# Round 0 of an RWKV-6 kernel: levels 0 and 1 and the diagonal as quarter products on TensorE

## The chip, the cores and the metric

The kernel runs on one core of one Trainium2 chip. A core has five engines that run their own instruction lists side by side: TensorE (PE, matrix products; its weight loads are shown as PEld), VectorE (DVE), ScalarE (ACT), GpSimd (POOL) and SyncE (SP, which here only issues DMA transfers). The metric is the device time of one execution in microseconds, as a median over runs. One more execution was recorded by the hardware profiler; its trace is what the views below are taken from.

## The reference

Everything is fp32. Batch B = 4, heads H = 8, steps S = 768, head size D = 48. First a recurrence over the steps, one 48x48 state per head:

```python
for t in range(S):
    cur = einsum('bhd,bhe->bhde', u[None] * k_t, v_t)
    y[:, :, t] = einsum('bhd,bhde->bhe', r_t, state + cur)
    state = w_t[:, :, :, None] * state + einsum('bhd,bhe->bhde', k_t, v_t)
```

Then y is brought into the form (4, 768, 384), called x, and goes through layer norm (with the gain g), a product with w_ch1 (384x1536), relu, a product with w_ch2 (1536x384), and x is added.

Written out over a stretch of steps, the output at step t is a sum over earlier steps s of v_s times the number A[s, t] = sum over d of k_s[d] r_t[d] times all w[d] strictly between s and t; for s = t the factor is u[d] instead; and what came before the stretch comes in through the state. The kernel works in that form: A is the matrix that this change is about.

## The kernel before

*Rounds.* The 4x768 steps are cut into 8 rounds of 384 steps (three tiles of 128 steps, TT = 3), each with all 8 heads. Two heads lie together in one turned operand (rows 0 to 47 and 64 to 111), which gives two units of two pairs. Within a round A is built for chunks of 64 steps (C = 64); the decays are multiplied up over six levels (NLEV = 6) of blocks of 1, 2, 4, 8, 16 and 32 steps.

*What a level does.* At level n, A's entries between a block of 2^n steps and the block that follows it are one product of k, already multiplied by the w up to the end of its block, and r, already multiplied by the w from the start of its block. `quads` (line 807) computes these as small TensorE products, 64 rows by 32 columns in PSUM (tile `a`), four of them on the four quadrants of the array; `keep` (868) copies what belongs to the level into A with a mask (DVE, copy_predicated), and for the last level `keep_last` (895) does so on ACT; `grow` (839, DVE) multiplies k and r by the totals of w, so that they fit the next level; `totals` (784) makes these totals by products of pairs.

*Below level 2.* The quarter products start at level 2 (LOW = 2). What lies within a block of four steps, that is levels 0 and 1 and the diagonal with u, is made from the inputs as loaded ("natural": step on the partitions, no transposing), in `inner` (570): elementwise products on DVE or POOL of nat_k, nat_r and nat_w, and sums over d into `vals`. It also leaves k and r, multiplied up to level 2, in the padded tiles pad_k and pad_r, and the product of four w in `w4`. `turn` (728) transposes pad_k and pad_r (four transposes of 128x112 into one PSUM bank, evicted by ACT or DVE into k and r); `turn_w` (756) does so with `w4`, into `tot`. `inner_by_tile` (670) sends `vals` to DRAM (own_d) and fetches it back in the layout of A (`va`): seven small transfers on SP for each part of a round. `place_own` (705) puts `va` into A with a mask.

*After A.* `turn_k`, `load_v`, `states`, `inside`, `outputs` (912 to 1133) make the products with v and the chain of states; `normalize` and `turn_x` (1134, 1225) the layer norm and its transposes; `first_product`, `mlp`, `halve` and `thirds` (1568, 1594, 1358, 1471) the two products of the metaformer, with `h_ps` the PSUM of the first one. The first rounds use fp32 weights. Later rounds use weights and activations split into parts (tiles whose names carry H, L and D); `thirds` issues the last rounds' second product, and ends with two DVE additions and a store for each tile of 128 steps.

*Weights.* They arrive as 8-byte words (`raw`, 384 KB each, on SP's queue) and are made into fp32 by ACT and DVE (`convert`, 1289). The first product cannot start before the first of them are done.

*Round 0.* It has two parts: its first tile alone, and the two others (`parts_of_round`, 512). Nothing else can run yet, so TensorE waits in it. `front` (1688) writes down all work of a part.

*What sets the order.* Every step is handed to a planner (class `Plan`) as an operation with an estimated cost, what it reads and what it writes. The order in which operations are issued is written out by hand as a list of their numbers (`ORDER`, line 76; ten thousand times n added where the n-th alternative engine is to do it). Each engine runs its own share of that list in that order. The planner's costs don't change the order, they only tell where TensorE is expected to wait for more than 0.35 us:

```python
if idle and e == "PE" and t - free["PE"] > 0.35:
    early = max(min(t - 0.1, self.WARMED) - free["PE"], 0.0)
    n = int(early / idle[1] / 2 + (t - 0.1 - free["PE"] - early) / idle[1])
```

There it issues products of zeros, `idle` (1783), n units of 128 columns, up to three units in one instruction. They are instructions like any other: once in the list they run. `busy` (1792) holds the times at which each engine is taken to be free at first. One helper issues every instruction, so all rows of the profile carry its line, L47; tiles tell them apart.

Of the kernel before, what the change touches and what calls it, by code (L numbers as in the profile page):

```python
# [63 lines left out]
class Plan:  # L64
# [294 lines left out]
def kernel(  # L359
# [18 lines left out]
    P = 128  # L378
# [349 lines left out]
    def turn(nm, part, c, stage):  # L728
        rnd, c0, nc = part
        name, ps = f"{nm}{rnd}", f"{nm}_ps{rnd}_{c}"  # L730
        pad = f"pad_{nm}{rnd}"

        def go():
            t = tile_("b", ps, [P, Q * P])
# [953 lines left out]
    def front(part):  # L1688
# [27 lines left out]
        for c in range(c0, c0 + nc):  # L1716
            for nm in "kr":
                turn(nm, part, c, 4 + "kr".index(nm))
# [106 lines left out]
```

## Time and profile before

| | us |
|---|---|
| median of 3 runs | 469.41 (468.7 to 469.71) |
| the profiled execution, whole | 469.36 |
| its span (first to last recorded instruction) | 467.6 |
| TensorE busy | 459.7 (98%) |
| VectorE busy | 352.5 (75%) |
| ScalarE busy | 264.5 (57%) |
| GpSimd busy | 139.1 (30%) |

The span leaves out 469.36 − 467.6 = 1.76 us that lie around it. A row of the timeline gives the start, the time from the first start to the last end, engine, line, operation, `output<-inputs`, the moving shape and the number of records (an fp32 product leaves two), and in brackets how long the engine stood idle before and what released it. Tile names: `k_ps`, `r_ps`, `w_ps` the turned inputs, `a` the quarter products and the products with v, `xT_ps` the turned x, `h_ps` the first product, `idle` the products of zeros.

### The profile page before, as it was taken

The page shows a single profiled execution, that of the slowest core. Times are in us where ns is not written, and L with a number is a line of the kernel's source. Part 1 is how long each engine was busy: PE and PEld are TensorE (multiplying, and loading weights), DVE is VectorE, ACT ScalarE, POOL GpSimd, SP SyncE. Part 2 cuts the span into 40 slices and gives each one's busy share as a digit, 9 for nine tenths or more (in the row PEclk, how much of TensorE's full clock was granted, in tenths as well). Part 3 has the DMA queues.
Part 4 walks back from the last instruction along what each step waited for, and adds up shares of the span by engine and source line. Part 5 has one row for each costly group of instructions (what it writes and reads, how often), then busy time and mean ns, then how long its engine had stood idle before and what let it go on. Part 6 is the DMA issues. An engine that isn't in the chain of part 4 may idle for free.

```text
span 467.6 us, 17460 instructions
## 1 busy us (share of the span) xinstructions
PE 459.7 (98%) x7442; PEld 400.8 (86%) x7442; DVE 352.5 (75%) x742; ACT 264.5 (57%) x608; POOL 139.1 (30%) x141
## 2 busy tenths in 40 slices
PE   9999999999999999999999999999999999999996
PEld 5766888766899766899766899999999999999996
DVE  8999899999997768897879887976633535525535
ACT  4697889754674332665621678855555455544440
POOL 4237014322361152363443230221013122321030
PEclk9999999999999999999999999999999999999999
DMA  7889765885657606844630545312212232142011
GB/s 207 248 199 240 203 124 144 239 212 139 180 160 162 133 4 151 185 128 127 170 66 4 86 123 133 105 32 69 84 55 70 80 102 67 37 135 68 35 50 51
DMA packets 105501, 56.23 MB, mean 120 GB/s; under 512 B 61904, under 2 KB 102352, under 8 KB 105424
## 3 DMA queue, kind: packets, MB, share of 16 engines
q1 hardware_dynamic: 105152, 54.92, 45.9%
q8 instruction: 58, 0.95, 0.9%
q10 hardware_dynamic: 272, 0.20, 0.1%
q14 instruction: 19, 0.16, 0.1%
HBM read 45.27 MB, written 7.47 MB: 113 GB/s over the span
## 4 chain that ended last, share of the span: by engine, by line
PE 86%; DVE 6%; DMA 3%; ACT 2%; POOL 2%; issue 1%; DVEq 0%; SPq 0%; POOLq 0%; ACTq 0%
PE h_ps L47 28%; PE a L47 25%; PE o L47 15%; PE o_2P L47 4%; PE idle L47 3%; PE r_ps L47 2%; PE k_ps L47 2%; PE o_2D L47 2%; DMA raw<-in_moe_w_ch_dram 2%; PE kn_ps L47 2%; PE xT_ps L47 2%; DVE s L47 1%; ACT held L47 1%; DMA va<-own_d 1%; POOL nat_k L47 1%
## 5 line engine op out<-in xcount | busy, mean ns | idle before, releaser
L47 ACT ACTIVATE h<-h_ps 128x384 f32<-128x384 f32 (+2 forms) x108 | 47.9, 457 | 50.5 <-PE h_ps L47 49.8
L47 PE MATMUL o<-ffn,h 128*128 128x384 f32 x216 | 74.6, 491 | 0.0
L47 DVE SCALAR_TENSOR_TENSOR hD<-hH,hL 128x384 fp32r<-128x384 f32 x60 | 36.4, 617 | 37.1 <-POOL hL L47 16.0
L47 POOL TENSOR_TENSOR hL<-h,hH 128x384 fp32r<-128x384 f32 x28 | 30.2, 1084 | 102.7 <-PE a L47 27.7
L47 ACT ACTIVATE h_ps<-h_ps 128x384 f32<-128x384 f32 x84 | 39.7, 480 | 34.5 <-PE h_ps L47 33.4
L47 PEld LDWEIGHTS o<-ffn,h 128*128 128x128 f32 x216 | 39.2, 190 | 23.0
L47 PEld LDWEIGHTS a<-r,k 48*56 48x56 f32 (+3 forms) x3072 | 40.0, 122 | 10.8 <-issue 5.2
L47 PE MATMUL h_ps<-xd,d 128*128 128x384 f32 x204 | 47.1, 335 | 0.0
L47 PE MATMUL a<-r,k 48*56 48x32 f32 (+3 forms) x3072 | 44.2, 208 | 1.0 <-issue 0.7
L47 PE MATMUL h_ps<-xhl,wl 128*128 128x384 f32 x180 | 40.4, 334 | 0.0
L47 DVE TENSOR_TENSOR r<-r,tot 112x768 f32<-112x768 f32 (+1 forms) x40 | 32.3, 809 | 9.6 <-PE a L47 9.6
L47 PE MATMUL h_ps<-xhl,wh 128*128 128x384 f32 x180 | 39.1, 326 | 0.0
L47 DVE TENSOR_TENSOR k<-k,tot 112x768 f32<-112x768 f32 (+1 forms) x40 | 31.6, 791 | 6.7 <-PE a L47 4.7
L47 ACT ACTIVATE hH<-h 128x384 fp32r<-128x384 f32 x60 | 29.7, 519 | 11.6 <-PE a L47 7.8
L47 PEld LDWEIGHTS h_ps<-xd,d 128*128 128x128 f32 x204 | 34.0, 189 | 0.5
L47 DVE TENSOR_TENSOR hL<-h,hH 128x384 fp32r<-128x384 f32 x32 | 18.0, 569 | 20.0 <-PE a L47 9.5
L47 PEld LDWEIGHTS h_ps<-xhl,wh 128*128 128x128 f32 x180 | 30.8, 189 | 0.0
L47 PE MATMUL idle<-nought 128*128 128x384 f32 (+2 forms) x90 | 29.6, 452 | 0.9 <-DVE eps L47 0.9
L47 ACT COPY A<-a 32x384 f32<-32x384 f32 (+5 forms) x56 | 23.6, 422 | 11.9 <-DVE xhl L47 5.6
L47 PEld LDWEIGHTS h_ps<-xhl,wl 128*128 128x128 f32 x180 | 30.1, 189 | 0.2
L47 PE MATMUL a<-w2D,hD 128*128 128x384 f32 x90 | 29.7, 330 | 0.4 <-DVE hD L47 0.4
L47 ACT ACTIVATE xf<-xT_ps,g_sb 128x384 f32<-128x384 f32 (+2 forms) x27 | 14.7, 550 | 22.1 <-PE xT_ps L47 19.0
(184 smaller groups left out, 1136.9 us busy)
## 6 DMA issues: line engine op xcount, KB each, us to landing
d<-w1d SPq DMA_DIRECT2D x84, 192.0 KB, 2.6
raw<-in_moe_w_ch_dram SPq DMA_DIRECT2D x24, 384.0 KB, 4.6
nat_w<-in_w_dram SPq DMA_DIRECT2D x24, 192.0 KB, 4.0
nat_r<-in_r_dram SPq DMA_DIRECT2D x24, 192.0 KB, 4.0
v<-in_v_dram SPq DMA_DIRECT2D x24, 192.0 KB, 4.1
nat_k<-in_k_dram SPq DMA_DIRECT2D x23, 192.0 KB, 4.1
out_dram<-x SPq DMA_DIRECT2D x15, 192.0 KB, 2.0
w1d<-w1diff SPq DMA_DIRECT2D x12, 192.0 KB, 2.3
```

The source lines that it names most:

```text
L47: ins = self.tc.keep_in_program_order(f(*args, **kw))
```

## The change

Round 0 has no `inner`, `turn_w`, `inner_by_tile` and `place_own` any more; rounds 1 to 7 keep them. In round 0

- `turn` takes nat_k, nat_r and nat_w as loaded. They have no padding, so the first head of a pair goes to rows 0 to 47 by a transpose of 64 columns, and the second to rows 64 to 111 by an fp32 product with the identity: four of each for a tile and an input. w is turned in the same way (before, only its products of four were).
- `totals` starts at level 0; the totals of levels 0 and 1 lie in pad_k0 and pad_r0, which round 0 no longer needs.
- `quads`, `keep` and `grow` run at level 1 too, and `grow` at level 0.
- the diagonal and level 0 are two new sets of products, `steps_alone`: with even columns (odd = 0) and odd ones (odd = 1). Their left operand `KU` (in the buffer of the second A) is k times u (`scale_k`), and for the odd columns the even steps of it are replaced by k itself (`even_k`). `keep_alone` copies them into A by two new masks.
- u is loaded a second time, as columns (`u_t`, two small transfers on ACT's queue).
- the second A is cleared after round 0 instead of at the start.

In the last round, `thirds` now splits the D part off for all three tiles (before, for the last one). `busy` for DVE is 5.4 instead of 4.4. The list `ORDER` is replaced as a whole (2187 entries instead of 2189); idle instructions fall from 45 to 26.

```diff
-    masks = {lev: const.tile([P, C // 2], I8, name=f"mask{lev}") for lev in range(LOW, NLEV - 1)}
+    masks = {lev: const.tile([P, C // 2], I8, name=f"mask{lev}") for lev in [*range(NLEV - 1), "odd"]}
+    u_t = const.tile([P, NA], F32, name="u_t")
...
+        raw = [(f"nat_{nm}{rnd}", c, i) for i in range(2)]
+        if nm == "w":
+            name = "pad_k0"
...
+            if rnd == 0:
+                src = tiles[f"nat_{nm}{rnd}"][:, c].rearrange("p j s d -> p (j s d)")
+                for s in range(Q):
+                    PE.transpose(t[0:HP, ts(s, P)], src[:, ds(s * D, HP)], ident)
+                    PE.matmul(t[HP:PD, ts(s, P)], src[:, ds((Q + s) * D, D)], ident, start=True, stop=True)
+                return
...
-            "PE", 0.437, go, count=2 * Q, r=[(pad, i, c0) for i in range(2)] + keys, w=[ps],
-            new=[("b", ps)] + ([(nm, name)] if c == 0 else []), pri=urgent(part, stage), lat=0.178,
+        keys = keys_of(nm, (rnd, c, 1)) if nm != "w" else [("pad_k0", 0, c)]
+        plan.add(
+            "PE", 0.437 if rnd else 1.3, go, count=2 * Q + 4 * Q * (rnd == 0),
+            r=([(pad, i, c0) for i in range(2)] if rnd else raw) + keys, w=[ps],
+            new=[("b", ps)] + ([(nm, name)] if c == 0 and nm != "w" else []), pri=urgent(part, stage), lat=0.178,
...
-        for lev in range(LOW, NLEV):
+        for lev in range(0 if rnd == 0 else LOW, NLEV):
...
+    def scale_k(part):
+        rnd, c0, nc = part
+        for a in range(NA):
+            def go(e, a=a):
...
+                    ACT.activation(out=to, in_=K[:, a], func=AF.Copy, scale=scale)
+                else:
+                    BY[e].tensor_scalar(out=to, in0=K[:, a], scalar1=scale, scalar2=None, op0=ALU.mult)
...
+    def even_k(part, us):
+        rnd, c0, nc = part
+        sl = slice(NP * us[0], NP * (us[-1] + 1))
+
+        def go(e):
+            K = of(part, tiles[f"k{rnd}"].rearrange("p u t -> p (u t)")[0:PD], P)
+            (ACT.copy if e == "ACT" else POOL.tensor_copy)(
+                out=of(part, KU[0:PD], P)[:, sl, 0::2], in_=K[:, sl, 0::2]
...
+    def steps_alone(part, odd, us=both_units):
+        rnd, c0, nc = part
+        name = f"a{rnd}_d{odd}_{c0}"
+
+        def go():
...
+                R = tiles[f"r{rnd}"][:, uu].rearrange("p (m q two) -> p m q two", m=NM, two=2)
+                for pr in pairs:
+                    for c in range(nc):
+                        for i in range(2):
+                            for j in range(2):
+                                m = 2 * (pr * TT + c0 + c) + i
+                                rows = ds(HP * j, D)
+                                PE.matmul(
+                                    to[ds(C * (i ^ j), C), j, uu, pr, c],
+                                    KU[rows, ds((uu * NM + m) * C, C)], R[rows, m, :, odd],
...
+    def keep_alone(part, odd):
+        rnd, c0, nc = part
+        name = f"a{rnd}_d{odd}_{c0}"
...
+            m = masks["odd" if odd else 0]
...
+            DVE.copy_predicated(out=to, data=ps, mask=m)
...
-            if last and rnd == NR - 1 and i == 2:
-
+            if last and rnd == NR - 1:
...
+            clear_a(0)
+        if rnd:
+            inner(part)
+            turn_w(part)
         for c in range(c0, c0 + nc):
-            for nm in "kr":
-                turn(nm, part, c, 4 + "kr".index(nm))
+            for nm in "kr" if rnd else "krw":
+                turn(nm, part, c, 4 + "krw".index(nm))
...
+            scale_k(part)
             for us in apart:
+                steps_alone(part, 0, us)
+                even_k(part, us)
+            keep_alone(part, 0)
+            for us in apart:
+                steps_alone(part, 1, us)
+            keep_alone(part, 1)
+        for lev in range(LOW if rnd else 0, NLEV):
+            for us in apart if lev else ():
                 quads(part, lev, us)
             for us in apart:
                 for nm in "kr":
                     grow(part, lev, nm, us)
-            if lev < NLEV - 1:
+            if 0 < lev < NLEV - 1:
...
-            place_own(part)
+        if rnd == 0 and c0 + nc == TT:
+            clear_a(1)
...
-    busy = {"PE": 1.0, "ACT": 1.0, "DVE": 4.4, "POOL": 2.5, "SP": 0.8}
+    busy = {"PE": 1.0, "ACT": 1.0, "DVE": 5.4, "POOL": 2.5, "SP": 0.8}
```

More of the change, by code (lines that the diff above doesn't have):

```diff
@@ L489 @@
     ACT.copy(out=a_homes[1], in_=nought[:, :, None].broadcast_to([P, 2, 512]))
-    for lev in range(LOW, NLEV):
-        n = 1 << lev if lev < NLEV - 1 else Q
-        blocks = const.tile([P, C // (2 * n if lev < NLEV - 1 else n)], F32, name=f"blocks{lev}")
+    DVE.memset(u_t, 0.0)
+    for lev in [0, "odd", *range(1, NLEV - 1), "own"]:
+        n = {"odd": 2, "own": Q}.get(lev) or 1 << lev
+        half = lev not in ("odd", "own")
+        blocks = const.tile([P, C // (2 * n if half else n)], F32, name=f"blocks_{lev}")
         ones = ident.rearrange("p (h q two n) -> p q two h n", h=2, two=2, n=n)[:, :, 0] if (
-            lev < NLEV - 1
+            half
         ) else ident.rearrange("p (h q n) -> p q h n", h=2, n=n)
         DVE.tensor_reduce(out=blocks, in_=ones, axis=AX.XY, op=ALU.max)
-        m = masks[lev].rearrange("p (q n) -> p q n", n=n) if lev < NLEV - 1 else own_mask
+        m = own_mask if lev == "own" else masks[lev].rearrange("p (q n) -> p q n", q=blocks.shape[1])
         DVE.tensor_copy(out=m, in_=blocks[..., None].broadcast_to(m.shape))
@@ L740, in keep @@
         def keep(e="ACT"):
-            to = tile_(nm, name, [P, U, W])[0:PD].rearrange("p u (r t) -> p (u r) t", r=NP)
+            if nm == "w":
+                to = level_total((0, 0, TT), 0)
+            else:
+                to = tile_(nm, name, [P, U, W])[0:PD].rearrange("p u (r t) -> p (u r) t", r=NP)
             to = to[:, :, ts(c, P)].rearrange("p a (k s) -> p a k s", s=Q)
@@ L786, in totals @@
         tot, dec = f"tot{rnd}", f"decay{rnd}"
-        for lev in range(LOW, NLEV):
+        for lev in range(0 if rnd == 0 else LOW, NLEV):
             def go(e, lev=lev):
+                tile_("tot", tot, [P, 2 * (U * W >> LOW)])
+                tile_("decay", dec, [P, U * NM])
                 pair = level_total(part, lev).rearrange("p a (q two) -> p a q two", two=2)
@@ L793, in totals, with total_keys @@
             plan.add(
-                EITHER, cost_of(nc * NA * P >> lev + 1), go, r=[(tot, lev, c0)],
-                w=[(tot, lev + 1, c0)] if lev < NLEV - 1 else [(dec, c0)], pri=urgent(part, 6 + lev),
-            )
+                EITHER, cost_of(nc * NA * P >> lev + 1), go, r=total_keys(part, lev),
+                w=total_keys(part, lev + 1) if lev < NLEV - 1 else [(dec, c0)],
+                new=[("tot", tot), ("decay", dec)] if c0 == 0 and lev == LOW - 1 else [],
+                pri=urgent(part, 6 + lev),
+            )
+    def total_keys(part, lev):
+        rnd, c0, nc = part
+        if lev < LOW:
+            return [(f"pad_{'kr'[lev]}0", 0, c) for c in range(c0, c0 + nc)]
+        return [(f"tot{rnd}", lev, c0)]
     def level_total(part, lev):
         rnd = part[0]
+        if lev < LOW:
+            t = tiles[f"pad_{'kr'[lev]}0"].rearrange("p s c j d -> p (s c j d)")
+            return of(part, t[0:PD, 0 : U * W >> lev], P >> lev)
         if lev == NLEV:
@@ L852, in go @@
             )
-        total = [(f"tot{rnd}", lev, c0)]
         plan.add(
-            "DVE", 0.15 + 0.4 * nu * nc / TT, go, r=total, w=keys_of(nm, part, us),
+            "DVE", 0.15 + 0.4 * nu * nc / TT, go, r=total_keys(part, lev), w=keys_of(nm, part, us),
             pri=urgent(part, 8 + 2 * lev), port=True,
@@ L893, in keep, with ku_keys @@
         )
+    KU = a_bufs[1].rearrange("p j u k t -> p (j u k t)")
+    def ku_keys(part, us=both_units):
+        return [("ku", a, part[1]) for uu in us for a in range(NP * uu, NP * (uu + 1))]
+    def scale_k(part):
[3 more added lines that the diff above has]
+                K = of(part, tiles[f"k{rnd}"].rearrange("p u t -> p (u t)")[0:PD], P)
+                to, scale = of(part, KU[0:PD], P)[:, a], u_t[0:PD, a : a + 1]
+                if e == "ACT":
+                    ACT.activation(out=to, in_=K[:, a], func=AF.Copy, scale=scale)
+                else:
+                    BY[e].tensor_scalar(out=to, in0=K[:, a], scalar1=scale, scalar2=None, op0=ALU.mult)
+            plan.add(
+                ("ACT", "DVE", "POOL"), (0.2 + 0.105 * nc, 0.15 + 0.07 * nc, 0.25 + 0.25 * nc), go, r=keys_of("k", part, [a // NP]) + [("u_t", j) for j in range(2)],
+                w=[("ku", a, c0)], pri=urgent(part, 6),
+            )
@@ new lines, in even_k @@
+    def even_k(part, us):
+        rnd, c0, nc = part
+        sl = slice(NP * us[0], NP * (us[-1] + 1))
+        def go(e):
+            K = of(part, tiles[f"k{rnd}"].rearrange("p u t -> p (u t)")[0:PD], P)
+            (ACT.copy if e == "ACT" else POOL.tensor_copy)(
+                out=of(part, KU[0:PD], P)[:, sl, 0::2], in_=K[:, sl, 0::2]
+            )
+        plan.add(
+            ("ACT", "POOL"), (0.2 + 0.105 * nc * len(us), 0.25 + 0.096 * nc * len(us)), go, r=keys_of("k", part, us), w=ku_keys(part, us),
+            pri=urgent(part, 7),
+        )
@@ new lines, in steps_alone @@
+    def steps_alone(part, odd, us=both_units):
+        rnd, c0, nc = part
+        name = f"a{rnd}_d{odd}_{c0}"
+        def go():
+            if us[0] == 0:
+                tile_("a", name, [P, 2, 512])
+            to = tiles[name].rearrange("s j (u r c t) -> s j u r c t", u=U, r=NP, t=C // 2)
+            for uu in us:
+                R = tiles[f"r{rnd}"][:, uu].rearrange("p (m q two) -> p m q two", m=NM, two=2)
[8 more added lines that the diff above has]
+                                    KU[rows, ds((uu * NM + m) * C, C)], R[rows, m, :, odd],
+                                    start=True, stop=True,
+                                )
+        share = len(us) * nc / TT
+        plan.add(
+            "PE", 0.05 + 0.68 * share, go, r=ku_keys(part, us) + keys_of("r", part, us),
+            w=[(name, uu) for uu in us], new=[("a", name)] if us[0] == 0 else [],
+            pri=urgent(part, 7), lat=0.2, tiled=True, count=round(96 * share),
+        )
@@ new lines, in keep_alone, with go @@
+    def keep_alone(part, odd):
+        rnd, c0, nc = part
+        name = f"a{rnd}_d{odd}_{c0}"
+        def go():
+            ps = tiles[name].rearrange("s j (a x) -> s (j a) x", a=NA)
+            ps = ps[:, :, 0 : nc * (C // 2)].rearrange("s b (c x) -> s b c x", c=nc)
+            to = a_bufs[rnd % 2].rearrange("s j u (r c) t -> s (j u r) c t", c=TT)[:, :, c0 : c0 + nc]
+            to = to.rearrange("s b c (x two) -> s b c x two", two=2)[..., odd]
+            m = masks["odd" if odd else 0]
+            m = m[:, None, None].broadcast_to([P, 2 * NA, nc, C // 2])
+            if nc == 1:
+                to, ps, m = to[:, :, 0], ps[:, :, 0], m[:, :, 0]
+            DVE.copy_predicated(out=to, data=ps, mask=m)
+        plan.add(
+            "DVE", cost(part, 0.155, 0.98), go, r=[(name, 0), (name, 1), (f"A{rnd % 2}", "nought")],
+            w=[(f"A{rnd % 2}", "alone", c0, odd)], pri=urgent(part, 8),
+        )
@@ L907, in keep_last @@
                     r=[(name, 0), (name, 1)] + [(f"A{rnd % 2}", 0, c0, j)] * (rnd > 0)
-                    + [(f"A{rnd % 2}", low, c0) for low in range(LOW, lev)],
+                    + [(f"A{rnd % 2}", low, c0) for low in range(LOW if rnd else 1, lev)]
+                    + [(f"A{rnd % 2}", "alone", c0, odd) for odd in range(2)] * (rnd == 0),
                     w=[(f"A{rnd % 2}", lev, c0, i, j)], pri=urgent(part, 21),
@@ L1067, in inside @@
             "PE", cost(part, 0.03, 0.73), go,
-            r=[(A_, lev, c0) for lev in range(LOW, NLEV - 1)] + [(A_, 0, c0, j) for j in range(2)]
+            r=[(A_, lev, c0) for lev in range(LOW if rnd else 1, NLEV - 1)]
+            + [(A_, 0, c0, j) if rnd else (A_, "alone", c0, j) for j in range(2)]
             + [(A_, NLEV - 1, c0, i, j) for i in range(2) for j in range(2)]
@@ L1685, in mlp, with clear_a, clear @@
         )
+    def clear_a(i):
+        def clear(e, i=i):
+            if e == "ACT":
+                ACT.copy(out=a_bufs[i], in_=nought[:, :, None, None, None].broadcast_to(a_bufs[i].shape))
+            else:
+                BY[e].memset(a_bufs[i], 0.0)
+        plan.add(
+            ("ACT", "POOL", "DVE"), (1.5, 1.8, 1.75), clear, w=[(f"A{i}", "nought")] + [key for part in parts_of_round(0) for key in ku_keys(part)] * i,
+            pri=-40,
+        )
     def front(part):
@@ L1729, in front @@
                     grow(part, lev, nm, us)
-            if lev < NLEV - 1:
+            if 0 < lev < NLEV - 1:
                 keep(part, lev)
         keep_last(part)
-        if rnd == 0:
-            place_own(part)
+        if rnd == 0 and c0 + nc == TT:
+            clear_a(1)
         for a in groups_of(part):
```

19 lines of the change are left out of this document (7 added, 12 removed), and 258 rows, old and new, of the table ORDER.

## The prediction

> **What bounds the kernel now.** I read the page's busy shares and slices first, then the chain, then windows of all engines, then TensorE's (PE's) own rows.
>
> ```profile
> PE 459.7 (98%) x7442; PEld 400.8 (86%) x7442; DVE 352.5 (75%) x742; ACT 264.5 (57%) x608; POOL 139.1 (30%) x141
> PE   9999999999999999999999999999999999999996
> DMA  7889765885657606844630545312212232142011
> PE 86%; DVE 6%; DMA 3%; ACT 2%; POOL 2%; issue 1%; DVEq 0%; SPq 0%; POOLq 0%; ACTq 0%
> ```
>
> PE is busy from end to end and is 86% of the chain. But "busy" hides filler, so I cut the span in four: up to PE's first real instruction (9.03 us), up to its first product of the metaformer (52.12), up to its last instruction, and the tail.
>
> ```profile
> 0.00:9.03 9.03, 8.10 (x16) 4.59 (x17) 6.76 (x21) 4.15 (x5) 5.33 (x16) 1.00 0.67 197
> 9.03:52.12 43.09, 41.04 (x897) 30.82 (x895) 41.09 (x106) 34.58 (x84) 15.69 (x14) 1.00 0.86 228
> 52.12:463.22 411.10, 410.57 (x6531) 365.35 (x6531) 303.31 (x614) 225.76 (x520) 118.12 (x111) 1.00 0.43 107
> 463.22:467.60 4.38, 0.00 (x0) 0.00 (x0) 1.31 (x3) 0.00 (x0) 0.00 (x0) 1.00 0.33 118
> ```
>
> The columns are length, then the busy time of PE, its weight loads, VectorE (DVE), ScalarE (ACT) and GpSimd (POOL), the clock, the DMA share and GB/s. From 52.12 on PE has work without a hole: 410.57 of 411.10. So whatever the change does is decided by when PE comes to that point, by what PE still owes there, and by the tail. The same windows for the tile "idle" alone (products of zeros that the planner put where it expects PE to wait) show how much of the first two is filler:
>
> ```profile
> 0.00:9.03 9.03, 8.10 (x16) 4.46 (x16) 1.00 0.67 197
> 9.03:52.12 43.09, 21.50 (x75) 12.21 (x74) 1.00 0.86 228
> ```
>
> Of 43.09 us, 21.50 are filler, 41.04 − 21.50 = 19.54 useful, and 43.09 − 41.04 = 2.05 empty. DVE is busy for 41.09 of them: in this stage it is the engine that PE waits behind, and the filler stands for DVE's time.
>
> **The change, part by part.** *Round 0's inner products leave DVE, and its 14 transfers through own_d leave SP.* On DVE that frees some 14 us before 41 us (the products and sums over nat_k, nat_r and nat_w, four copies of va into A) and adds about 8 (four copies of the new masks, one level's keep, two levels of k and r times totals). These rows price it:
>
> ```profile
> 14.37 0.42 DVE L47 TENSOR_TENSOR k<-k,tot 112x256 f32<-112x256 f32 x1
> 14.71 0.42 DVE L47 TENSOR_TENSOR r<-r,tot 112x256 f32<-112x256 f32 x1
> 22.57 0.70 DVE L47 COPY_PREDICATED A<-mask,a 128x512 f32<-128x512 int8 x1
> ```
>
> Starts lie 0.34 apart. DVE's relief itself gives nothing: PE now has more to do, so PE's list sets when the stage ends. If that is wrong, DVE's order prevails, which rival 2 prices. The extra masks on DVE (three more pairs) and u_t's two small loads on ACT's queue lie ahead of the first eviction, while inputs are in flight: nothing, and at most 0.5 us if the first eviction waits. Clearing the second A later is work for ACT, POOL or DVE ahead of round 1, when none of them ends last: nothing.
>
> *PE's list up to its first h_ps product.* In the program as built, six turns of four transposes and three turns of w go; nine turns of raw tiles come, each with four transposes (64 rows) and four fp32 products with the identity (48 rows), which run as two passes each. Three levels of 48 quarter products come (16 of the first tile, 32 of the others). Round 1's 48 first quarter products now stand behind the first h_ps.
>
> ```profile
> 9.03 0.60 PE L47 MATMUL k_ps<-ident,pad_k 128*112 128x128 f32 x4
> 9.47 1.03 PE L47 MATMUL idle<-nought 128*128 128x384 f32 x4
> 14.13 0.40 PE L47 MATMUL w_ps<-ident,w 128*112 128x128 f32 x2
> 12.30 0.64 PE L47 MATMUL a<-r,k 48*60 48x32 f32 x32 [0.17 <-ACT r L47]
> 12.87 1.35 PE L47 MATMUL idle<-nought 128*128 128x384 f32 x4
> 20.73 1.00 PE L47 MATMUL a<-r,k 48*48 48x32 f32 x64
> 21.66 1.14 PE L47 MATMUL idle<-nought 128*128 128x384 f32 x4
> 58.40 0.60 PE L47 MATMUL xT_ps<-ident,xn 128*128 128x128 f32 x4
> 58.84 1.50 PE L47 MATMUL h_ps<-xf,w 128*128 128x128 f32 x12
> 60.18 0.38 PE L47 MATMUL xT_ps<-ident,xn 128*128 128x128 f32 x2
> ```
>
> Four transposes occupy 9.47 − 9.03 = 0.44 us (0.11 each). Twelve passes of 128 columns take 60.18 − 58.84 = 1.34 (0.11 each), with no cost where transposes and products meet. A raw turn has 4 + 8 = 12 passes of 128 columns: 1.33 us if they follow one another. If each transpose ran beside its two passes, on the other half of the columns, it would be 8 × 0.11 = 0.89. What speaks for that:
>
> ```profile
> 36.74 0.25 PE L47 MATMUL a<-v,A 64*64 64x48 f32 x1 [0.30 <-DVE s L47]
> 36.76 0.25 PE L47 MATMUL a<-vx,A 64*64 64x48 f32 x1
> 36.83 0.22 PE L47 MATMUL a<-v,A 64*64 64x48 f32 x1
> ```
>
> Four products on the array's four quadrants start within 0.02 us. But these share neither rows nor columns with each other in pairs, and no row shows two products side by side that both use all 128 rows. The raw turn reads 128 rows, as h_ps and xT_ps do, so I take 1.33 and keep 0.89 for the range. Sum: 9 × 1.33 = 11.97, less 6 × 0.44 and 0.34 for w (three transposes), is +9.0. Quarter products: 12.87 − 12.30 = 0.57 for the first tile and 21.66 − 20.73 = 0.93 for the others, 1.5 a level, three levels: +4.5. Moved behind h_ps: −1.4 (48 products at the 1.5 of a level, a little less by the shorter form). Useful work: 19.54 + 9.0 + 4.5 − 1.4 = 31.6.
>
> *Filler.* The new list has 45 − 26 = 19 fewer idle instructions. In units of 128 columns: before 23 ahead of the first real instruction and 74 behind it; after, 5 and 48. At 21.50 / 74 = 0.29 a unit the 48 take 13.9. They run whether or not PE would have waited.
>
> *Start.* The first turn needs only a raw nat_r, now first on SP's queue.
>
> ```profile
> 0.74 0.76 SPq L47 DMA_DIRECT2D nat_w<-in_w_dram  x1
> 1.56 0.62 SPq L47 DMA_DIRECT2D nat_r<-in_r_dram  x1
> 5.08 0.36 DVE L47 TENSOR_TENSOR rk<-nat_k,nat_r 128x192 f32<-128x192 f32 x1 [0.61 <-DMA nat_r<-in_r_dram]
> ```
>
> It landed 5.08 − 1.56 = 3.5 us after its issue, so 0.74 + 3.5 = 4.24 us. Against 9.03 that is the largest gain. PE is still slow then:
>
> ```profile
> 6.21 0.34 PEld L47 LDWEIGHTS idle<-nought 128*128 128x128 f32 x1 [0.30 <-issue]
> 6.85 0.64 PEld L47 LDWEIGHTS idle<-nought 128*128 128x128 f32 x2 [0.30 <-issue]
> ```
>
> A pass of 384 columns takes 0.64 until 6.85 and half of it afterwards, as the row at 12.87 shows, so PE loses half of 6.85 − 4.24: 1.3 us.
>
> *Empty time.* The 2.05 contain 0.30 ahead of the products of 36.74 (row above), a state behind the copies of va that go: 1.75 is left. With POOL gone from the path the rest could shrink (to nothing: −1.75), or a new wait come; I keep it.
>
> *Sum.* First h_ps at 4.24 + 1.3 + 31.6 + 13.9 + 1.75 = 52.8 (52.12 before). Then 411.10, the 1.4 moved into it, and the tail.
>
> *Tail.* The last second-product now has its D part split off for every tile, and both DVE additions follow the last product.
>
> ```profile
> 462.89 0.33 PE L47 MATMUL a<-w,hH 128*128 128x384 f32 x1
> 463.31 0.61 DVE L47 SCALAR_TENSOR_TENSOR x<-a,rstdD,x 128x384 f32<-128x384 f32 x1
> 463.95 0.62 DVE L47 SCALAR_TENSOR_TENSOR x<-a,rstd,x 128x384 f32<-128x384 f32 x1
> ```
>
> Both additions already follow it, so 4.38 stays; were one moved ahead it would be −0.6.
>
> 52.8 + 411.1 + 1.4 + 4.4 = 469.7 against 467.6: +2.1 on the profiled execution, 467.6 + 1.76 = 469.36, itself 0.05 under the median of the three runs (469.41). Forecast 471.4 us.
>
> **Rivals.** *1, the other side: the halves overlap.* Place: the nine raw turns; price 9 × 0.44 = 4.0 less, 467.4 us, if all of it reaches the end. It decides from 2.1 us saved on. For it: the quadrants. Against it: 128 rows in both, and two operations. [...] Chance 0.17.
>
> *2, overlap, but weights hold the gain back.* ACT converts weights in list order, and raw_266 stands ahead of the scaling of k for tiles 1 and 2. Ahead of it on the queues are nine inputs of 192 KB and four weights of 384 KB (itself included): 3.34 MB.
>
> ```profile
> 0.00:5.00 5.00, 4.07 (x7) 2.26 (x8) 1.00 0.46 136
> 5.00:10.00 5.00, 4.73 (x13) 2.70 (x12) 1.00 0.92 270
> 10.00:15.00 5.00, 3.73 (x13) 2.05 (x12) 1.00 0.95 267
> ```
>
> 136, 270 and 267 GB/s over 5 us each are 3.37 MB at 15 us. With some 3 us of ACT's conversions, scalings and one eviction behind it, the diagonal products of tiles 1 and 2 start at about 18.4; in my sum PE reaches them at about 20.2 (4.24 + 1.3 + 12.0 for the turns, 1.7 for three groups of the first tile, 1 filler and wait). Only 1.8 of the 4.0 is then won: 469.6 us, no change. Against it: landings follow only roughly from bytes. Chance 0.27.
>
> *3, the clock stays halved for longer.* After five units of filler (about 2.1 us from 0.93) PE pauses until 4.24. If the 5.9 us that warming took (0.93 to 6.85) start over, the slow time ends at 10.15, and half of 3.3 is lost besides: +1.7, 473.1 us. Against it: the pause is short. [...] Chance 0.10.
>
> **How the numbers follow.** Forecast 0.43, rivals 0.17, 0.27 and 0.10, and 0.03 for none of these. About 0.2% (0.94 us) is what a measurement of this kernel tells from no change. Slower: forecast, rival 3 and a part of the rest, less what their lower bounds (the empty time, the tail) bring back to no change: 0.55. Faster: rival 1 and parts of 2: 0.21. Same: 0.24. Range 466.9 to 473.4: from rival 1, with 0.5 of the empty time gone too, to rival 3 with a little more of the fill's or the start's error; the forecast's own is 470.0 to 472.6.
>
> **What would show it.** PE's first real row r_ps at about 4.3, and its row at 0.44 (transposes) plus 0.88, or 0.89 in all, for each turn behind 7 us: this one reading decides between forecast and rivals 1 and 2. The idle tile with 48 units, about 14 us, behind it; the first h_ps at 52.8; then about 412.5 us of full PE; a tail of 4.4. If the wait ahead of the diagonal products of tiles 1 and 2 ends on ACT behind held<-raw, it is rival 2. The prediction is wrong if the first h_ps comes before 51 us, or if the stretch behind it is not 411 + 1.4.

## The result: 8% slower, and the profile after

| | before | after |
|---|---|---|
| median | 469.09 us (4 runs) | 507.21 us (4 runs, 505.83 to 508.01) |
| ratio | | 1.0795, 95% interval 1.0761 to 1.0829 |
| span of the profiled execution | 467.6 us | 504.0 us |
| first h_ps product | 52.05 us (cut at 52.12 in the prediction) | 80.70 us |

The forecast was 471.4 us. Times are medians; where the runs of one kernel fall into two groups (two kernels below), the median is that of the faster group, and the others are given beside it. The page of the changed kernel looks as full as the one before:

```profile
PE 492.3 (98%) x7773; PEld 414.9 (82%) x7773; DVE 360.2 (71%) x743; ACT 267.8 (53%) x614; POOL 129.3 (26%) x142
PE   8999999999999979999999999999999999999996
PE 84%; DVE 8%; ACT 3%; DMA 2%; issue 1%; SPq 0%; POOL 0%; POOLq 0%; ACTq 0%; DVEq 0%
```

The same four stretches as in the prediction, cut at the changed kernel's own marks (first turn, first h_ps, last product), and the stretch of round 0 for the tile idle alone:

```profile
0.00:4.24 4.24, 2.50 (x5) 1.21 (x5) 3.01 (x17) 2.40 (x3) 1.82 (x11) 1.00 0.43 129
4.24:80.70 76.46, 76.25 (x1143) 45.82 (x1144) 45.17 (x113) 35.84 (x84) 7.99 (x17) 1.00 0.48 139
80.70:499.44 418.74, 413.26 (x6628) 367.82 (x6627) 310.55 (x613) 229.59 (x529) 119.50 (x114) 1.00 0.41 106
499.44:503.96 4.52, 0.33 (x3) 0.03 (x1) 1.51 (x3) 0.00 (x0) 0.00 (x0) 0.89 0.35 126
```

```profile
4.24:80.70 76.46, 17.97 (x48) 9.42 (x48) 1.00 0.48 139
```

Against the prediction's 52.8 us for the first h_ps and 416.9 us behind it (411.1 + 1.4 + 4.4), 27.9 us are lost ahead of it and 423.3 − 416.9 = 6.4 us behind it. PE's timeline shows the first loss at once:

```profile
4.24 3.82 PE L47 MATMUL r_ps<-ident,nat_r 128*64 128x128 f32 x12 [0.82 <-DMA nat_r<-in_r_dram]
7.99 7.63 PE L47 MATMUL w_ps<-ident,nat_w 128*64 128x128 f32 x24
15.55 7.63 PE L47 MATMUL k_ps<-ident,nat_k 128*64 128x128 f32 x24
41.26 0.80 PE L47 MATMUL idle<-nought 128*128 128x128 f32 x2
59.50 0.49 PE L47 MATMUL idle<-nought 128*128 128x128 f32 x2
```

The start is as predicted (4.24). But two raw turns take 15.55 − 7.99 = 7.56 us, 3.78 each, where 1.33 was forecast. And the same instruction of idle takes 0.80 at 41 us and 0.49 at 59: the clock is still halved at 41 us. The clock record of the trace begins at full clock only at 55.85 us (before the change: 7.10). The clock column of the windows does not show this, since it is empty ahead of that first record; the lengths of equal instructions do.

Single records inside one raw turn, at half clock:

```profile
15.55 0.42 PE L47 MATMUL k_ps<-ident,nat_k 128*64 128x128 f32 x1
15.90 0.45 PE L47 MATMUL k_ps<-ident,nat_k 128*48 128x128 f32 x1
16.14 0.42 PE L47 MATMUL k_ps<-ident,nat_k 128*48 128x128 f32 x1
16.50 0.42 PE L47 MATMUL k_ps<-ident,nat_k 128*64 128x128 f32 x1
```

From the first pass of a product (128*48) to its second it is 0.24 us; from a transpose (128*64) to the product and back to a transpose 0.35 and 0.36. So something is paid at each border between the two kinds, and there are eight of them in a turn.

### The profile page after: what moved, and what is told of

It reads as the page before. It is cut to its first block, busy times and chain, and to the rows that moved or that the text cites. A ratio compares the mean times of both kernels' runs of the same rounds, so it can differ in the third digit from the quotient of the medians.

```text
span 504.0 us, 18109 instructions
## 1 busy us (share of the span) xinstructions
PE 492.3 (98%) x7773; PEld 414.9 (82%) x7773; DVE 360.2 (71%) x743; ACT 267.8 (53%) x614; POOL 129.3 (26%) x142
## 4 chain that ended last, share of the span: by engine, by line
PE 84%; DVE 8%; ACT 3%; DMA 2%; issue 1%; SPq 0%; POOL 0%; POOLq 0%; ACTq 0%; DVEq 0%
PE h_ps L47 27%; PE a L47 26%; PE o L47 9%; PE k_ps L47 4%; PE o_2P L47 4%; PE r_ps L47 4%; PE w_ps L47 3%; PE idle L47 3%; PE o_2D L47 2%; PE kn_ps L47 2%; PE xT_ps L47 2%; DVE nat_k L47 1%; DVE k L47 1%; DVE A L47 1%; DVE vals L47 1%; DMA own_d<-vals 1%
## 5 line engine op out<-in xcount | busy, mean ns | idle before, releaser
L47 DVE SCALAR_TENSOR_TENSOR hD<-hH,hL 128x384 fp32r<-128x384 f32 x60 | 37.6, 646 | 46.4 <-POOL hL L47 21.6
L47 POOL TENSOR_TENSOR hL<-h,hH 128x384 fp32r<-128x384 f32 x32 | 34.0, 1067 | 110.1 <-PE a L47 24.7
L47 PEld LDWEIGHTS o<-ffn,h 128*128 128x128 f32 x216 | 39.2, 190 | 22.1
L47 PEld LDWEIGHTS a<-r,k 48*60 48x60 f32 (+4 forms) x3168 | 43.3, 128 | 12.7 <-issue 4.4
L47 PE MATMUL a<-r,k 48*60 48x32 f32 (+4 forms) x3168 | 47.6, 213 | 3.0 <-DVE A L47 2.7
L47 PE MATMUL h_ps<-xhl,wl 128*128 128x384 f32 x180 | 41.5, 340 | 0.0
L47 DVE TENSOR_TENSOR k<-k,tot 112x768 f32<-112x768 f32 (+1 forms) x40 | 33.4, 839 | 7.7 <-PE a L47 4.3
L47 ACT COPY A<-a 32x384 f32<-32x384 f32 (+5 forms) x60 | 24.9, 425 | 7.4 <-PE a L47 6.8
L47 PE MATMUL a<-w2L,hL 128*128 128x384 f32 x80 | 26.1, 326 | 0.0
```

Of the source, the lines that this page charges most:

```text
L47: ins = self.tc.keep_in_program_order(f(*args, **kw))
```

## The experiments

**Borders, pause or narrow weights.** Four kernels change the raw turn, or what comes ahead of it. The first writes both heads by transposes only, and changes `go` in `turn`:

```diff
-PE.transpose(t[0:HP, ts(s, P)], src[:, ds(s * D, HP)], ident)
-PE.matmul(t[HP:PD, ts(s, P)], src[:, ds((Q + s) * D, D)], ident, start=True, stop=True)
+PE.transpose(t[0:PD, ts(s, P)], src[:, ds((Q + s) * D - HP, PD)], ident)
+PE.transpose(t[0:HP, ts(s, P)], src[:, ds(s * D, HP)], ident)
```

> The raw turn of round 0 is made of two transposes for each step (the second head's first, 112 columns wide, then the first head's over it, 64 wide) instead of a transpose and a product on the upper half of the columns: no column-half products, so no border between the two kinds, 8 passes instead of 12. Theory A (borders: every change between a transpose and a column-half product costs about 0.14 us at half clock, and the gaps keep the clock halved until 55 us): a turn falls from 3.78 to 0.9 us, full clock by 10 us, first h_ps at 47 to 52 us, time 466 to 471. Theory B (the pause before nat_r keeps the clock halved, whatever the turns are): turns of 1.8 us, clock still halved beyond 40 us, time above 485. Theory C (narrow weights are slow by themselves): the 64-wide transposes stay slow, turns of about 2 us, time 480 to 495.

The second puts the four transposes ahead of the four products (two loops over s instead of one):

> Same twelve passes in each raw turn, but the four transposes first and the four column-half products after them: two borders a turn instead of eight. Theory A: a turn of about 2.9 us at half clock (12 x 0.22 + 2 x 0.14), PE's gaps small enough for full clock early, then about 1.5 us; time 472 to 480. Theory B: 2.9 us throughout, clock halved beyond 40 us, time about 498. Theory C: 3.78 us as before, time 507.

The third has full-width products, so no half of the columns is ever used:

```diff
-PE.transpose(t[0:HP, ts(s, P)], src[:, ds(s * D, HP)], ident)
-PE.matmul(t[HP:PD, ts(s, P)], src[:, ds((Q + s) * D, D)], ident, start=True, stop=True)
+PE.matmul(t[0:PD, ts(s, P)], src[:, ds((Q + s) * D - HP, PD)], ident, start=True, stop=True)
+PE.transpose(t[0:HP, ts(s, P)], src[:, ds(s * D, HP)], ident)
```

> Twelve passes as in the changed kernel, but the identity products of the second head over all 112 columns, from row 0 on, and then the first head's transposes over their lower rows: no column halves. That is the turn that the prediction had priced. Theory A: 1.33 us a turn at full clock, full clock by 10 us, time 469 to 474. Theory B: 2.7 us a turn, clock halved beyond 40 us, time above 490. Theory C: as A, since half of the weights are wide, but with the 64-wide transposes slow: 480 to 495.

The fourth leaves the turns alone and adds 18 units to the first idle group (`n += 18` for the first group):

> The changed kernel with 18 more units of idle products at the very start, as many as before the change, so that PE is busy without a pause from 0.9 to about 9 us and the first raw turn begins at full clock. Theory A: the first one or two turns take about 1.9 to 2.2 us (12 x 0.11 and eight borders), then the clock is halved again and turns take 3.78; time 505 to 513. Theory B: the clock stays full, all turns below 2.2 us, time 480 to 490. Theory C: turns slow at full clock too, about 1.9, clock stays full: 480 to 490.

A fifth has the two loops over pairs of steps, so four borders a turn:

> The changed kernel with two transposes, then two column-half products in each half of a turn: four borders a turn, between eight (the changed kernel) and two. If a border has a fixed price, a turn takes 1.33 + 4 x 0.125 = 1.83 us at full clock, or 3.25 at half. Clock: at half clock 2.67 of these 3.25 us are passes (82%), against 71% with eight borders, where it rose only at 55 us, and 90% with two, where it rose at 6.2. If it rises before 12 us: time 485 to 490. If not: 497 to 503.

Rows of PE's timeline at full clock, in the order: eight borders (with the early filler), four, two, none (full-width products), none (two transposes). The start of the next row less that of the first is the time of two turns. (Some clock times in the expectations are about 1 us too early; the table has those of the record.)

```profile
10.26 4.70 PE L47 MATMUL w_ps<-ident,nat_w 128*64 128x128 f32 x24
14.89 0.30 PE L47 MATMUL k_ps<-ident,nat_k 128*64 128x128 f32 x1
```

```profile
11.86 3.70 PE L47 MATMUL k_ps<-ident,nat_k 128*64 128x128 f32 x24
15.49 0.76 PE L47 MATMUL w_ps<-ident,nat_w 128*64 128x128 f32 x4
```

```profile
10.28 3.19 PE L47 MATMUL k_ps<-ident,nat_k 128*64 128x128 f32 x24
13.40 0.87 PE L47 MATMUL w_ps<-ident,nat_w 128*64 128x128 f32 x5
```

```profile
9.43 2.78 PE L47 MATMUL k_ps<-ident,nat_k 128*112 128x128 f32 x24
12.05 1.47 PE L47 MATMUL w_ps<-ident,nat_w 128*112 128x128 f32 x12
```

```profile
8.92 1.91 PE L47 MATMUL k_ps<-ident,nat_k 128*112 128x128 f32 x16
10.66 1.04 PE L47 MATMUL w_ps<-ident,nat_w 128*112 128x128 f32 x8
```

| raw turn | passes | borders | us at full clock | over 1.31, per border | clock full from | time |
|---|---|---|---|---|---|---|
| changed kernel's, early filler | 12 | 8 | 2.315 | 0.126 | 5.0 us, lost at 35.7 | 502.4 |
| in pairs | 12 | 4 | 1.815 | 0.126 | 9.4 us | 485.4 |
| grouped | 12 | 2 | 1.56 | 0.125 | 7.2 us | 485.0 |
| full-width products | 12 | 0 | 1.31 | | 6.9 us, lost at 27.4 | 481.4 |
| two transposes | 8 | 0 | 0.87 | | 8.4 us, lost at 18.6 | 483.7 (482.7 to 486.4); three others 490.3 to 494.0 |
| changed kernel | 12 | 8 | 3.78 at half | 0.145 at half | 55.85 us | 507.2 |

("Clock full from" is the start of the first stretch at full clock in the trace's clock record, in us from the start of the span; "lost" is its next halving ahead of the first h_ps. The trace of the two-transposes kernel is that of its longest run.) The price of a border is the same in three kernels, 0.126 us, and the passes cost what the prediction said (1.31 against 1.33, 0.87 against 0.89). Theory A's price stands on this. Theory B, that the pause alone keeps the clock halved, falls: the four kernels without early filler and with fewer borders pause in the same place, and their clock is full by 9.4 us. Theory C falls: 64-wide transposes are as quick as others (eight passes, four of them 64 wide, take 0.87 us, 0.11 each).

Theory A was wrong in one point. With early filler the clock did not fall back: it was full for 30.7 us, through all nine turns with eight borders, although in the turns the passes were then only 1.31 / 2.315 = 57% of the time. So the gaps did not halve the clock; at half clock, where passes are 2.62 / 3.78 = 69%, it did not rise in the turns. With four borders (2.62 of the 3.13 us that its first turn took, 84%) it rose. The late rise thus took both, the pause behind a short filler and the borders: with either of them gone the clock was full early. And the borders end with the last raw turn at 40.3 us; from there to 55.85 us the changed kernel's list is quarter products and filler, and no run shows why the clock stayed halved through these 15.6 us. The runs of the two-transposes kernel spread from 482.7 to 494.0 us, with a mean clock of 0.987 to 0.996 in the three shorter ones and 0.972 to 0.976 in the three longer; its shorter turn gained nothing over full-width products in either.

Of the first four times three lie above what theory A gave for them, by 5 us and more: it knew nothing of the stretch behind the first h_ps, the next question. The early filler came out below its 505 to 513, since the clock held. The fifth kernel's 485.4 lies in its forecast.

Ahead of the first h_ps the grouped, full-width and early-filler kernels came to 58.4, 56.2 and 70.4 us, against 80.7. Of the 10.3 us that the early filler gained there, 4.8 reached the time: behind the first h_ps its clock was halved for 10.2 us more, from 179.0 to 189.3 us.

**The stretch behind the first h_ps.** Even with full-width products it was 480.6 − 56.15 = 424.4 us (tail included), not 416.9. In the changed kernel the one long wait of PE there, and what DVE and ACT did ahead of it (timelines of PE, DVE and ACT):

```profile
187.19 1.52 PE L47 MATMUL a<-r,k 48*60 48x32 f32 x96 [2.66 <-DVE A L47]
```

```profile
184.55 1.01 DVE L47 COPY_PREDICATED A<-mask_own,va 128x768 f32<-128x768 int8 x1 [4.50 <-ACT A L47]
186.20 0.94 DVE L47 COPY_PREDICATED A<-mask,a 128x768 f32<-128x768 int8 x1
```

```profile
182.14 0.59 ACT L47 COPY k<-k_ps 112x512 f32<-112x512 f32 x1
182.61 1.90 ACT L47 COPY A<-a 16x384 f32<-16x384 f32 x4
```

The new order gives round 3's copy of level 4 to ACT (four copies of 16 rows), where it stands behind an eviction of k; DVE's `place_own` into the same A waits for it, and with it the next copy, for which PE waits. Behind that pause the clock is halved from 189.0 to 192.4 us; a window over the first 2.7 us of it has a mean clock of 0.59:

```profile
188.40:191.70 3.30, 3.01 (x124) 2.87 (x117) 2.46 (x4) 0.00 (x0) 0.04 (x1) 0.59 0.64 160
```

One entry of the order gives that copy to DVE (before the change it was DVE's):

```diff
-10906
+906
```

> The kernel with full-width products in its turns, and one entry of the order changed: round 3's copy of level 4 into A is done by DVE, not by ACT. Theory D (the stretch behind the first h_ps is longer because that copy stands behind late h_ps evictions on ACT, DVE's copy of va into the same A waits 4.5 us for it, PE stands 2.7 us and its clock is then halved for one or two stretches of 3.4 us): the wait of 2.7 us and the halved clock at about 163 us go, the stretch behind the first h_ps falls from 424.4 to about 419 to 421, time 475 to 478. Rival E (the wait is for va's transfer or anything else that comes late with the new order): DVE waits at the same place all the same, the time stays at 480 to 482.

479.39 us (4 runs); ratio to the kernel before 1.0205 (1.0186 to 1.0224). The wait and the halved clock are gone; the copy now runs on DVE, and place_own behind it:

```profile
158.60 0.99 DVE L47 COPY_PREDICATED A<-mask,a 128x768 f32<-128x768 int8 x1 [1.45 <-PE a L47]
159.96 1.02 DVE L47 COPY_PREDICATED A<-mask_own,va 128x768 f32<-128x768 int8 x1
162.03 1.52 PE L47 MATMUL a<-r,k 48*60 48x32 f32 x96
163.48 1.14 PE L47 MATMUL idle<-nought 128*128 128x384 f32 x4
```

The last row is new too: with this entry the planner expects a wait there and puts in six units of filler, so the run alone does not tell whether the copy or the filler holds the clock. Two kernels further down that have no filler behind the first turn tell it. With the copy on ACT the wait is there, and the clock is halved from 164.3 to 171.1 us; with the copy on DVE (and a part of round 1 left out) the wait is gone, and the clock is full from 52.2 us to the end of PE's work:

```profile
163.89 3.75 PE L47 MATMUL a<-r,k 48*60 48x32 f32 x192 [2.67 <-DVE A L47]
```

```profile
164.39 1.02 PE L47 MATMUL a<-r,k 48*32 48x32 f32 x96 [0.80 <-DVE k L47]
```

So the copy is enough.

The stretch behind the first h_ps fell by 4.5 us, to 477.6 − 57.66 = 419.9, as theory D said. The median fell by only 2 us, which two runs of the kernel with the copy on ACT (480.31 and 482.46) hardly settle, and in the traces by 3.0: the first h_ps came 1.5 us later in this execution (57.66; clock full from 9.5 us instead of 6.9, and 1.7 us of pauses that the list of waits puts down to issue, against 0.3). The total was forecast at 475 to 478, and missed that. The same entry alone, in the changed kernel:

> The changed kernel, raw turns as they are, with only round 3's copy of level 4 into A done by DVE. If the two causes add up: the wait of 2.7 us at about 187 us and the halved clock behind it go, 4 to 5 us less than 507.2: 502 to 503.5. If the wait belongs to the turns' lateness: 507.

504.37 us, 2.8 less and a little above what was expected; behind the first h_ps 502.4 − 83.07 = 419.3 instead of 423.3. Its clock rose only at 61.4 us, which took back a part. So the late copy costs about 4 us with either turn, apart from the borders.

**Filler.** The prediction put 13.9 us of filler on PE's path. Without it (full-width products, the copy on ACT, no idle product behind the first turn):

> The kernel with full-width products in its turns, without any idle product behind the first turn (48 units fewer, 13.9 us in the prediction's sum; the output is the same). Theory F (filler is on PE's path, as the prediction's sum has it, and DVE would be ready earlier): first h_ps at about 43 to 46 us, time 468 to 472. Rival G (filler only stands where PE waits for DVE, busy for 95% of 20 to 56 us): PE waits instead of it, the first h_ps moves by less than 2 us for that; and as PE's pauses halve the clock, everything around takes longer: first h_ps at 56 to 64, time 481 to 489.

485.73 us, first h_ps at 56.46. The windows up to 24 us and from there to the first h_ps:

```profile
4.00:24.00 20.00, 18.51 (x344) 17.26 (x344) 13.98 (x33) 10.79 (x24) 2.89 (x7) 1.00 0.83 247
24.00:56.46 32.46, 26.12 (x754) 23.28 (x751) 31.42 (x82) 25.74 (x63) 5.31 (x12) 0.58 0.62 177
```

The time is as rival G has it, but the clock (0.58 in the second window) confounds the reason: it could be DVE, busy for 31.42 of 32.46, or PE's useful work at half clock. So DVE's list was cut, with and without filler, both with the copy on DVE. What was left out, on DVE and for round 1: the products of nat_k with nat_r and u, those of pad_k with pad_r, and the three sums into vals.

> The kernel of the copy-on-DVE run, without round 1's products of nat_k with nat_r and u and of pad_k with pad_r on DVE, and without round 1's three sums into vals (this part of round 1's output is left out): 5.1 us of DVE's list ahead of the first layer-norm statistics, and 1.9 us behind them, ahead of the first h_ps. Theory H (behind the first tile DVE's list, busy from 19 to 56 us, sets the first h_ps, and the filler only fills PE's waits for it): the first h_ps comes 2 to 4 us earlier than 57.7 us, until PE's list with its filler is the bound; time 474 to 477. Rival I (PE's list, filler in it, sets the first h_ps, as the prediction's sum had it): the first h_ps stays within 1 us, time 478 to 480.

> The same, and without the 48 units of filler behind the first turn. Theory H: without filler DVE is the bound again, 5 to 7 us of its list are gone, so the first h_ps comes 3 to 7 us earlier than the 56.5 us of the run without filler (50 to 53 us), though PE's pauses still halve its clock; time 478 to 484. Rival I: PE's list without 13.9 us of filler would have set 43 to 46 us already in the run without filler; taking work from DVE changes nothing, 56 us.

482.88 us (479.47 and 486.29) and 481.35 us, first h_ps at 58.01 and 57.53. Up to there DVE is busy for 42.72 us instead of 47.46, and for 42.80 instead of 48.17 without filler, some 5 us less, and the first h_ps came no earlier. (The time without filler fell by 4.4 us, all of it behind the first h_ps, where the copy now runs on DVE.) Theory H falls, as far as the clock lets it: in the run with filler the clock was halved for 3.4 us from 34.0 us on, which can hide up to 1.7 us. With the filler kept, DVE now stands and waits for PE:

```profile
45.06 0.32 DVE L47 COPY s<-a 112x48 f32<-112x48 f32 x2 [1.75 <-PE a L47]
```

With half the filler in both kernels, full-width products and two transposes:

```diff
+n = n if count == self.BEFORE else (n + 1) // 2
```

> The kernel of the copy-on-DVE run (full-width products in the raw turns) with each filler group behind the first turn cut to half, rounded up: about 18 units fewer, 5.2 us in the prediction's sum. Open is whether filler lies on the path to the first h_ps; the run without any filler could not tell, since its clock was halved. Theory I (PE's list sets the first h_ps, filler in it): with the clock full, the first h_ps comes 4 to 5 us earlier than 57.7 (52.5 to 54), time 474 to 476. Rival J (the chain from PE to DVE and ACT and back sets it; filler fills PE's waits): pauses take the filler's place, first h_ps within 1.5 us of 57.7, time 478 to 481. If the clock is halved for long stretches, the run does not tell.

> The same halved filler with two transposes for a step in the raw turns, five units halved to three ahead of the first tile's level 1, and the copy on DVE: PE's list is another 4 us shorter. Theory I with a full clock: first h_ps at 48 to 51 us, time 469 to 473, level with the kernel before the change. Rival J: first h_ps at 54 to 56, time 477 to 480, or later where PE's pauses halve the clock.

484.74 and 484.40 us, first h_ps at 62.57 and 62.00, later than with all filler. Windows of the first of them, ahead of the point at which its clock is lost (26.06 us) and behind it:

```profile
8.60:25.60 17.00, 16.41 (x333) 14.61 (x332) 12.13 (x30) 11.91 (x26) 2.88 (x7) 1.00 0.79 225
25.70:56.30 30.60, 30.53 (x623) 22.30 (x616) 25.16 (x61) 19.39 (x47) 4.38 (x8) 0.51 0.54 152
```

PE is busy for 30.53 of 30.60 us at a clock of 0.51: it is PE's list that takes the time, and the list has grown by the halved clock. What the filler buys here is the clock: the four kernels with less of it had the clock halved for 27 us or more ahead of the first h_ps, the three with full-width products and all of it for 3.4 us or not at all. Whether PE, at full clock and with less filler, would wait for DVE stays open, since no such kernel kept the clock.

**A version to beat both.** Two transposes, the turn's cost told to the planner (0.95 us instead of 1.3), five units where PE had paused, and the copy on DVE:

> An attempt at a better version: two transposes for a step in the raw turns (as in the first experiment), the turn's cost told to the planner as 0.95, five units of filler where PE had paused ahead of the first tile's level 1 (the clock had been halved from 17.5 us there), and round 3's copy by DVE. If the clock now stays full: turns of 0.96, first h_ps at 50 to 53 us, stretch behind it about 420, time 472 to 476. If the pauses at other places still halve it: first h_ps at 56 to 60, time 478 to 485.

479.81 us (478.7 to 480.9; a fourth run 486.0): first h_ps at 55.31, clock lost for two stretches of 3.4 us, from 26.9 and 153.2 us. No version came below 478.7; the kernel before stays the fastest.

## Why the prediction was wrong, step by step

- *The raw turn, taken as twelve passes of 0.11 us: the step that failed.* The passes are right (1.31 us of them, measured). What was left out is the border: the turn was priced "with no cost where transposes and products meet", read from xT_ps and h_ps, both on full columns. Here the product sits on the upper half of the columns, and each change costs 0.126 us: 9 turns x (2.315 − 1.33) = 8.9 us. The three kernels with eight, four and two borders give that price (0.126, 0.126 and 0.125 us); what the array does at a border is not shown. Nor do the turn's records show the two halves side by side: transpose, the product's two passes and the next transpose start one after the other (15.55, 15.90, 16.14 and 16.50 us in the rows above).
- *The clock, put at half until 6.85 us.* It was halved until 55.85. On the turns that costs 9 x (3.78 − 2.315) = 13.2 us. On the filler and the small products it costs most of what is left: the filler took 17.97 instead of 13.9. Turns 22.1, filler 4.1 and the products of tile a 4.3 (21.75 us against 14.35 + 4.5 − 1.4) make 30.5; less 1.5 us of empty time that was not there and the 1.3 us that the prediction had counted for the slow clock, 27.7 of the 27.9 are accounted for. Rival 3 had the clock and half of the cause: it blamed PE's pause at 3.4 to 4.2 us. All kernels with fewer borders have that pause and a full clock by 10.1 us; the kernel with early filler has all borders, no pause, and a full clock from 5.0 us. Both together kept it halved through the turns; rival 3 had put the end at 10.15 us. In the changed kernel 36 us of raw turns with eight borders (and two groups of quarter products), with passes for 69% of a turn, went by without a rise; what makes the clock rise is not shown.
- *Rivals 1 and 2* (halves that overlap): no run shows it.
- *The start at 4.24*: right. *The tail at 4.4*: 4.2, from the end of PE's last product (499.77) as in the prediction; the window above begins with that product.
- *Full PE behind the first h_ps*: 6.4 us too little. Some 4 to 4.5 of them are one wait and its halved clock, from an entry of the new order that the prediction never looked at; it read the new list only ahead of the first h_ps.
- *What is left when both are mended*: 479.4 against 471.4. First h_ps at 57.66, not 52.8: 0.2 of start, 1.2 of slow clock (until 9.5), 1.0 of filler (14.86), 1.0 of empty time (2.74), and about 1.5 of useful work that was priced too low. Behind it 3.0 us; 2.5 of them are PE's empty time, 415.54 − 412.50 = 3.0 up to 473.2 us against 0.5 before the change, with these waits:

```profile
PE k_ps L47 <- POOL pad_k L47: 1.4, 1, 1.4
PE a L47 <- DVE x L47: 0.8, 1, 0.8
PE k_ps L47 <- DVE x L47: 0.4, 1, 0.4
PE kn_ps L47 <- DVE k L47: 0.4, 1, 0.4
```

- *DVE's relief of some 6 us (14 freed, 8 added)*: not seen. Up to the first h_ps DVE is busy for 47.46 us in the mended kernel and for 47.85 before. It was not the bound, so this did not count; how much of it is work of round 1 that moved ahead is not known.
- The sign was right, with 0.55 on slower, and holds for the mended kernel too (2% slower). The size was wrong by a factor of 19 (38.1 us against 2.0). The 2.0 us were a balance of other terms than those that made the loss, so the sign is in part luck.

## What to carry to other kernels

A price read from two instructions that follow one another holds only for that pair: if a new sequence changes the part of the array in use at each step, count the changes and price them (here 0.126 us each, a little more than a pass of 128 columns at 0.11). Group such work, or do it over all columns even if half the result is thrown away: twelve full-width passes took 1.31 us where the alternating ones took 2.3. And look at how long a known instruction takes in the first microseconds: the busy row reads 9 throughout, while the whole list may run at half clock, and filler that seems to cost 14 us may be what holds the clock (without it the clock was halved for 27.3 us here).

## What was not expected of the hardware

- No single threshold on the share of time that passes take fits the clock. With 69% at half clock it did not rise in 36 us of raw turns; with 57% at full clock it did not fall from 8 to 30 us, the time of its nine turns. Once lost among quarter products and filler, it came back after 3.4 us in three kernels (full-width products, less on DVE, the last version), but only after 10.2 us (early filler), 13.7 (two transposes), 27.3 (no filler) or 30.7 (half the filler) in others, although in the last of these the profile calls PE busy for 30.53 of 30.60 us. What decides between short and long is not shown.
- Masked copies into every second column, or into every second pair of columns, take almost twice as long (1.30 and 1.29 us against 0.71). In the kernel with full-width products, DVE's timeline:

```profile
25.63 1.30 DVE L47 COPY_PREDICATED A<-maskodd,a 128x512 f32<-128x512 int8 x1
26.73 0.40 DVE L47 TENSOR_SCALAR w<-w 128x384 int32<-128x384 int32 x1
27.36 1.29 DVE L47 COPY_PREDICATED A<-mask,a 128x512 f32<-128x512 int8 x1
33.93 0.71 DVE L47 COPY_PREDICATED A<-mask,a 128x512 f32<-128x512 int8 x1
34.53 0.55 DVE L47 CUSTOM_DVE_ANT_0 w<-w,held 128x768 uint16<-128x768 uint16 x1
```

  Start to start it is 1.10 us for the first (odd columns) and 0.60 for the copy at 33.93, of as many elements at level 2 (runs of four columns). The copy at 27.36 is that of level 1, in runs of two. The prediction had priced all of them by one of level 2.
